# Key sums of a linear-attention block: three column blocks summed with 32-column weights of ones, four token tiles in four partition quarters

## The chip, the core and the metric

The kernel runs on one core of one Trainium2 chip. The metric is the time of one execution in microseconds on the device; the median of three runs is used. A profiled execution has a span (first to last instruction) and a time of its own, which also holds what lies around the span.

## What is computed

A transformer block on 2048 tokens of width 640: layer norm, linear attention with 32 heads of 20, residual, layer norm, a gated MLP of width 1728, residual. The kernel computes the output and the gradients of the input and of five weight matrices. What matters here is one sum in the attention:

```
pq, pk = phi(q), phi(k)               # phi(t) = where(t > 0, t + 1, exp(t)) + 1e-6
kv  = einsum("bhsd,bhse->bhde", pk, v)
z   = einsum("bhsd->bhd", pk)         # key sums: over all 2048 tokens, one number per column
num = einsum("bhqd,bhde->bhqe", pq, kv)
den = einsum("bhqd,bhd->bhq", pq, z)[..., None] + 1e-6
o   = num / den
```

`z` has 640 numbers. The denominators need it beside every token, so it is wanted as a row of 640, the same in all 128 partitions.

## The kernel before

Tokens lie in 16 tiles of 128 (`ST = 16`), the width in 5 column blocks of 128 (`DT = 5`). `pk_all` holds phi of the keys, 128 tokens in the partitions, 16 tiles x 640 columns in each. The order of the work on every engine is written out by hand.

The loop at L521 to L564 goes over the 16 token tiles: it computes the keys on TensorE (`p1_mm`, L267), phi on ScalarE and VectorE, and in between some of the queries and the products `macc` (`m_part`, L422: `pk` transposed times the normalized input). Behind the loop, L579 to L630 finish `macc` block by block, while the queries and the first denominators are computed.

The key sums come in two ways. For blocks 0 and 1, `x_ext` carries a column of ones behind the input (memset at L447), so that the products of L422 give the sums as one more column of the accumulator; `m_end` copies that column to `Z` (L431). For blocks 2, 3 and 4, `z_late` (L330) makes them with matmuls of its own: for each of 16 token tiles and 3 blocks, the 128x128 tile of `pk_all` is loaded as weights and one column of ones moves through (L334). The three sums come out as three columns, one number per partition. ScalarE copies them to `Z` (L336).

`z_diag` (L326) then spreads each column of `Z` on a diagonal: VectorE multiplies the identity by it (L328) into a region of `hx`. `z_rows` (L340) multiplies a 128x128 matrix of ones by each diagonal (L344), which gives the row of sums in all partitions; ScalarE copies the rows to `Zb` (L347). The products `pq * Zb` (`r_prod`, L359, on GpSimd) and the sums over heads (`r_red`, L366, on VectorE) follow.

The order around the change:

```
579  q_tile(4)
...
582  phi_rest()
583  m_part(1, (14, 15))
584  m_end(1)
...
589  z_late((2, 3, 4), big())
590  m_part(2, range(10))
591  z_rows(((0, 1), (2, 3, 4)), ps.tile([P, 2, 512], F32, name="bigx", tag="big", bufs=2))
592  r_prod(0)
593  q_tile(5)
```

The accumulators of `m_part(2)` are the two of block 0 again (L419), so its first matmuls wait until ScalarE has copied these out (L429, L431). Later steps that the prediction speaks of: the weight product `Wp`, made on TensorE (`f2_wT`, L696), copied by ScalarE and VectorE (L699) and transposed by DMA on SyncE's queue (L700); the transposes of the scaled queries (`r_T`, L377); and the last column tile of the MLP gradient (`ghh_chunk`, L401), where 64 weight columns are used at a time and two halves of the tokens go to partitions 0 to 63 and 64 to 127 of one accumulator.

Of the kernel before, what the change touches and what calls it, by code (L numbers as in the profile page):

```python
# [9 lines left out]
P = 128  # L10
BF16 = mybir.dt.bfloat16
# [9 lines left out]
ST, DT = S // P, D // P  # L21
# [34 lines left out]
def kernel(  # L56
# [19 lines left out]
    V, A, T, G, SY = nc.vector, nc.scalar, nc.tensor, nc.gpsimd, nc.sync  # L76
# [27 lines left out]
    def pool(name, side="left", space=None):  # L104
        kw = dict(space=space) if space is not None else dict(side=side)
        return tc.alloc_tile_pool(name=name, bufs=1, reuse_waits="tile", **kw)

    cp = pool("cp")
# [10 lines left out]
    ones = cp.tile([P, P], BF16, name="ones")  # L119
# [115 lines left out]
    pk_all = p1.tile([P, ST, D], BF16, name="pk_all", tag="pk")  # L235
    mT = U1.tile([P, DT, D], BF16, name="mT", tag="MW")
    Z = cp.tile([P, DT], F32, name="Z")
# [14 lines left out]
    def p1_tr(t, parts=((0, DT),)):  # L252
        xn = x_sb[:, t, :]
        for a, b in parts:
            tr = ps.tile([P, DT, P], BF16, name="tr", bufs=2)
            for c in range(a, b):
                T.transpose(tr[:, c, :], xn[:, c * P:(c + 1) * P], ident[:])

            A.copy(out=pqT[:, a:b, t * P:(t + 1) * P], in_=tr[:, a:b, :])  # L259
# [13 lines left out]
    def p1_mm(t, n0, between=None, halves=None):  # L273
        acc = p1_acc() if halves is None else None
        for j in range(2):
            p1_half(acc[:, j, 0:HD] if halves is None else halves[j][:, 0:HD], t, n0 + j * HD)
            if j == 0 and between is not None:
                between()
        return acc
# [27 lines left out]
    hx = ph.tile([P, FT * W], BF16, name="hx", tag="H1")[:, 0:11 * D].rearrange("p (t n) -> p t n", n=D)  # L307
# [14 lines left out]
        phi(p1_mm(t, 0), pqs[t], t)  # L322

    dz = {}

    def z_diag(m):  # L326
        dz[m] = hx[:, 10, m * P:(m + 1) * P]
        V.tensor_scalar(out=dz[m], in0=ident[:], scalar1=Z[:, m:m + 1], scalar2=None, op0=ALU.mult)  # L328

    def z_late(ms, acc):  # L330

        for t in range(ST):
            for i, m in enumerate(ms):
                T.matmul(acc[:, i:i + 1], lhsT=pk_all[:, t, m * P:(m + 1) * P], rhs=ones[:, 0:1],  # L334
                         start=(t == 0 and i == 0), stop=(t == ST - 1), skip_group_check=True)
        A.copy(out=Z[:, ms[0]:ms[-1] + 1], in_=acc[:, 0:len(ms)])  # L336
        for m in ms:
            z_diag(m)

    def z_rows(parts, acc):  # L340

        for k, ms in enumerate(parts):
            for i, m in enumerate(ms):
                T.matmul(acc[:, k, i * P:(i + 1) * P], lhsT=ones[:], rhs=dz[m], start=(i == 0), stop=True,  # L344
                         skip_group_check=True)
        for k, ms in enumerate(parts):
            A.copy(out=Zb[:, ms[0] * P:(ms[-1] + 1) * P], in_=acc[:, k, 0:len(ms) * P])  # L347
# [173 lines left out]
    for t in range(ST):  # L521
        first = None
        if t < RAW:
# [11 lines left out]
            k = p1_mm(t, D, between, kh)  # L535
            act(0, 1)
            act(1, 1)
        else:
            k = p1_mm(t, D, (lambda: p1_tr(t + 1)) if t + 1 < XT_DMA else None)
# [47 lines left out]
    for go in w13[4:]:  # L587
        go()
    z_late((2, 3, 4), big())
    m_part(2, range(10))  # L590
    z_rows(((0, 1), (2, 3, 4)), ps.tile([P, 2, 512], F32, name="bigx", tag="big", bufs=2))
    r_prod(0)
    q_tile(5)
# [384 lines left out]
    for c in range(SC):  # L978
# [9 lines left out]
        for fc in range(FT):  # L988
# [23 lines left out]
            if c == SC - 1 and fc in (1, 2, 5, 6):  # L1012
                i = (1, 2, 5, 6).index(fc)
# [61 lines left out]
    for fc in range(FT - 1):  # L1075
        b, i = divmod(fc, 4)
        if fc == FT - 2:
            gw2_tail()
        acc = ps.tile([P, 2, 512], F32, name="gw", bufs=4)
        for j in range(2):  # L1080
            for t in range(ST):
                T.matmul(acc[:, j, 0:HD], lhsT=hb[b][:, t, i * P:(i + 1) * P], rhs=g2[:, t, j * HD:(j + 1) * HD],  # L1082
                         start=(t == 0), stop=(t == ST - 1))
# [35 lines left out]
    def b_ghn(t):  # L1119

        acc = ps.tile([P, 2, 512], F32, name="ghn", bufs=2)
        n = 0
        lo = (t % 2) * P
        for k in range(NG):
            rhs = wT[0][:, k, :] if k < FT else wT[1][:, k - FT, :]
            for j in range(2):
                T.matmul(acc[:, j, 0:HD], lhsT=ggb[t // 2][:, k, lo:lo + P], rhs=rhs[:, j * HD:(j + 1) * HD],  # L1127
                         start=(k == 0), stop=(k == NG - 1))
                n += 1
                if n % 9 == 0 and n < 54:  # L1130
                    yield
        b_ln(acc, t)
# [109 lines left out]
    for t in range(ST):  # L1242
        g = b_ghn(t)
# [13 lines left out]
        if t >= 1:  # L1257
# [3 lines left out]
            if t <= 2 * DT:  # L1261
                n = (t - 1) % DT
# [95 lines left out]
    def d_acc():  # L1358
        return ps.tile([P, 2, 512], F32, name="dkv", bufs=3)

    def square(lhsT, rhs, i):

        acc = d_acc()
        for c, a, b, bank, off, first in SQ:
            T.matmul(acc[:, bank, off:off + (b - a) * DH], lhsT=lhsT[:, c, i * P:(i + 1) * P],
                     rhs=rhs[:, c, a * DH:b * DH], start=first, stop=True, skip_group_check=True)
        return acc
# [12 lines left out]
    for m, (a, b) in enumerate(M_H):  # L1380
        n = (b - a) * DH
        acc = ps.tile([P, 512], F32, name="gkvT", tag="dkv", bufs=3)
        for c in range(DT):
            T.matmul(acc[:, 0:n], lhsT=woT[:, c, m * P:(m + 1) * P], rhs=QT[:, c, a * DH:b * DH], start=(c == 0),
                     stop=(c == DT - 1))
# [38 lines left out]
    acc = d_acc()  # L1424
    for m in range(DT):
        T.matmul(acc[:, m // 4, m % 4 * P:(m % 4 + 1) * P], lhsT=ones[:], rhs=gzd[:, m, :], start=(m % 4 == 0),
                 stop=True, skip_group_check=True)
# [3 lines left out]
    for t in range(ST):  # L1431
        c, i = divmod(t, TPC)
        u = t // 2
        acc = d_acc()
        for j in range(2):
            for k in range(DT):
                T.matmul(acc[:, j, 0:HD], lhsT=xnT[c][:, k, i * P:(i + 1) * P], rhs=gm[:, k, j * HD:(j + 1) * HD],  # L1437
                         start=(k == 0), stop=(k == DT - 1))
# [7 lines left out]
        if t in (2, 5, 8, 11, 14):  # L1446
            n = t // 3
            acc = square(mN, gkv_b, n)
            k = (4, 0, 1, 2, 3)[n]
# [7 lines left out]
        if t in (6, 8, 10, 12):  # L1457
            n = t // 2 - 3
# [20 lines left out]
    def both_grads(m, f0, f1):  # L1479

        return [(max(f0, lo) - f0, min(f1, lo + F) - f0, out[:, m, max(f0, lo) - lo:min(f1, lo + F) - lo])
                for lo, out in ((0, out4S), (F, out5S)) if max(f0, lo) < min(f1, lo + F)]
# [55 lines left out]
    for i, (f0, f1) in enumerate(blocks):  # L1538
        n = f1 - f0
        for m in range(DT):  # L1540
            last = (i, m) == (len(blocks) - 1, DT - 1)
            for a, b in ((0, n - P), (n - P, n)) if last else ((0, n),):
                c = (a + b) // 2
                halves = ((a, c), (c, b)) if i * DT + m < 6 else ((a, b),)
                out = [(x + y - a, z + y - a, to) for y, w in halves for x, z, to in both_grads(m, f0 + y, f0 + w)]
# [38 lines left out]
```

## Time and profile before

| what | value |
|---|---|
| median of 3 runs | 821.91 us (821.35 to 822.22) |
| profiled execution | 822.18 us, its span 820.4 us |
| TensorE matmuls (PE) | 812.7 us busy, 5437 instructions |
| TensorE weight loads (PEld) | 512.9 us busy, 5464 instructions |
| VectorE (DVE) | 453.0 us busy |
| ScalarE (ACT) | 325.3 us busy |
| GpSimd (POOL) | 131.0 us busy |
| DMA | 157.57 MB, mean 192 GB/s |

PE and PEld overlap: a weight load can run while a matmul streams. Busy time of PE counts overlapping matmuls once. The chain of work that ended last is followed back from the last instruction, at each step to what released it or to the instruction before it on its engine; its pieces are listed with start and length. In groups of instructions "128*128 128x320" is a matmul with weights of 128 rows by 128 columns whose output is 128 partitions by 320 columns. Some matmul records can be missing from a trace.

### The profile page before, as it was taken

What the parts mean: (1) busy time and instruction counts of PE and PEld (TensorE: products, weight loads), DVE (VectorE), ACT (ScalarE), POOL (GpSimd) and SP (SyncE); (2) the same over time, 40 slices, a digit from 0 to 9 for tenths busy, and PEclk for the clock granted to TensorE, in tenths of its full rate; (3) what the DMA queues carried; (4) which work ended last, traced back from release to release, by engine and by line L of the source; (5) the groups of instructions that cost most, each with busy time, mean ns of one, the idle gap of its engine ahead of it and who ended that gap; (6) DMA issues with size and microseconds to landing.
All of it is one profiled execution on the core that took longest, in us unless ns stands there. A gap on an engine that the chain in (4) does not pass through costs nothing.

```text
span 820.4 us, 14028 instructions
## 1 busy us (share of the span) xinstructions
PE 812.7 (99%) x5437; PEld 512.9 (63%) x5464; DVE 453.0 (55%) x976; ACT 325.3 (40%) x605; POOL 131.0 (16%) x193
## 2 busy tenths in 40 slices
PE   8999999999999999999999999999999999999998
PEld 6677544555555545777777777777777777544444
DVE  7859887999898566300057777772781544200000
ACT  7856788655565666011122212222212334211111
POOL 2233333323322212100001111110220000000000
PEclk9999999999999999999999999999999999999999
DMA  9999989696485556999777897359996898978761
GB/s 231 252 271 237 210 233 321 191 240 156 140 218 156 159 188 167 223 263 257 220 173 178 207 204 187 72 113 180 240 210 125 166 197 158 238 166 191 167 138 37
DMA packets 322690, 157.57 MB, mean 192 GB/s; under 512 B 241728, under 2 KB 315872, under 8 KB 322624
## 3 DMA queue, kind: packets, MB, share of 16 engines
q1 hardware_dynamic: 279712, 115.85, 63.5%
q10 hardware_dynamic: 35584, 16.34, 9.3%
q0 software_dynamic: 7328, 24.48, 8.9%
q8 instruction: 43, 0.70, 0.4%
q14 instruction: 23, 0.19, 0.1%
HBM read 47.09 MB, written 51.13 MB: 120 GB/s over the span
## 4 chain that ended last, share of the span: by engine, by line
PE 95%; DMA 3%; DVE 1%; ACT 1%; issue 0%; SPq 0%; DVEq 0%
PE mm L387 20%; PE job L1331 20%; PE ghn L1127 14%; PE gxn L1500 8%; PE gw L1082 7%; PE o L895 4%; PE o L841 3%; PE big L267 3%; PE gwo L1215 3%; PE gr L1184 3%; PE dkv L1437 3%; PE macc L422 2%; PE at L648 2%; PE mm L267 1%; DMA pqT<-pql 1%; DMA wqkv<-in_A_wqkv_dram 1%
## 5 line engine op out<-in xcount | busy, mean ns | idle before, releaser
L1331 PE MATMUL job<-gb,hnN 128*128 128x496 bf16 (+3 forms) x576 | 116.8, 366 | 0.0
L1127 PEld LDWEIGHTS <-ggb 128*128 128x128 bf16 x864 | 84.5, 98 | 32.9
L1331 PEld LDWEIGHTS <-hnN 128*128 128x128 bf16 x576 | 55.7, 98 | 61.1
L387 PE MATMUL mm<-pqT,w 128*128 128x512 bf16 x397 | 93.2, 379 | 0.5
L387 PEld LDWEIGHTS <-w 128*128 128x128 bf16 x540 | 52.5, 98 | 63.1 <-issue 1.1
L1335 ACT CAST obs<-job 128x496 bf16<-128x496 f32 (+4 forms) x56 | 28.5, 509 | 123.7 <-PE job L1331 123.7
L1127 PE MATMUL ghn<-w13a,ggb 128*128 128x320 bf16 x448 | 63.5, 299 | 0.0
L1142 DVE SCALAR_TENSOR_TENSOR wb<-gs,hnb 128x640 f32<-128x640 bf16 x16 | 13.2, 826 | 89.8 <-ACT gs L1139 89.8
L1127 PE MATMUL ghn<-w13b,ggb 128*128 128x320 bf16 x416 | 61.4, 299 | 0.0
L387 PE MATMUL mm<-g2T,w2T 128*128 128x512 bf16 x227 | 58.5, 379 | 0.6
L1082 PE MATMUL gw<-g,hb 128*128 128x320 bf16 x416 | 56.8, 299 | 0.0
L1192 POOL TENSOR_TENSOR sz<-Zb,g_h 128x640 f32<-128x640 bf16 x16 | 20.2, 1260 | 197.7 <-DVE g_h L1193 197.7
L1082 PEld LDWEIGHTS <-hb 128*128 128x128 bf16 x416 | 40.6, 98 | 16.0 <-issue 0.3
L412 ACT CAST ghh<-mm 128x512 bf16<-128x512 f32 x48 | 28.3, 589 | 43.5 <-PE mm L387 36.8
L778 ACT ACTIVATE sig<-mm 128x512 bf16<-128x512 f32 x56 | 33.7, 602 | 25.7 <-PE mm L387 22.0
L1139 ACT ACTIVATE gs<-ghn 128x640 bf16<-128x640 f32 x16 | 11.2, 703 | 78.8 <-PE ghn L1127 58.4
L387 PEld LDWEIGHTS <-w2T 128*128 128x128 bf16 x260 | 25.3, 98 | 23.3
L267 PEld LDWEIGHTS <-pqT 128*128 128x128 bf16 x320 | 30.4, 98 | 14.2 <-ACT pqT L259 0.9
L267 PE MATMUL big<-wqkv,pqT 128*128 128x320 bf16 x250 | 38.4, 299 | 0.5 <-DMA pqT<-x_sb 0.3
L1331 PEld LDWEIGHTS <-g 128*128 128x128 bf16 x320 | 31.0, 98 | 11.6
L814 DVE TENSOR_TENSOR gate<-gate,sig 128x1024 bf16<-128x1024 bf16 x28 | 19.3, 690 | 33.7 <-ACT gate L789 33.6
L789 ACT CAST gate<-mm 128x512 bf16<-128x512 f32 x56 | 33.6, 600 | 4.1 <-DMA gg_d<-gate 4.0
(216 smaller groups left out, 1372.7 us busy)
## 6 DMA issues: line engine op xcount, KB each, us to landing
hh_d<-hhT SPq DMA_DIRECT2D x24, 256.0 KB, 2.8
gg_d<-gate POOLq DMA_DIRECT2D x24, 256.0 KB, 4.6
gg_d<-ghh POOLq DMA_DIRECT2D x24, 256.0 KB, 3.9
ggb<-gg_d SPq DMA_DIRECT2D x6, 896.0 KB, 5.3
ggb<-gg_d ACTq DMA_DIRECT2D x6, 832.0 KB, 5.7
x_sb<-in_A_x_dram SPq DMA_DIRECT2D x6, 640.0 KB, 5.7
ggb<-gg_d SPq DMA_DIRECT2D x2, 1728.0 KB, 12.7
pk_d<-pk_all SPq DMA_DIRECT2D x4, 640.0 KB, 8.0
```

The lines of the kernel that those rows point to most:

```text
L267: T.matmul(acc, lhsT=pqT[:, c, t * P:(t + 1) * P], rhs=wqkv[:, c, n0:n0 + HD], start=(c == 0), stop=(c == DT - 1))
L387: T.matmul(acc[:], lhsT=w[:, c, fc * P:(fc + 1) * P], rhs=rhs[:, c, :], start=(c == 0), stop=(c == DT - 1))
L412: A.copy(out=ghh[n // 2][:, n % 2, :], in_=acc[:])
L778: A.activation(sig[:, i, :], gp[:], AF.Sigmoid)
L789: A.copy(out=gate[:, i, :], in_=gp[:])
L841: T.matmul(accs[i, j][:, 0:HD], lhsT=hhT[c][:, fc, i * P:(i + 1) * P], rhs=w2[:, fc, j * HD:(j + 1) * HD], start=(first and fc == 0), stop ...
L895: T.matmul(o2["ps"][:, 0:HD], lhsT=hhT[c][:, fc, i * P:(i + 1) * P], rhs=w2[:, fc, j * HD:(j + 1) * HD], start=(fc == 0), stop=(fc == FT - 1))
L1082: T.matmul(acc[:, j, 0:HD], lhsT=hb[b][:, t, i * P:(i + 1) * P], rhs=g2[:, t, j * HD:(j + 1) * HD], start=(t == 0), stop=(t == ST - 1))
L1127: T.matmul(acc[:, j, 0:HD], lhsT=ggb[t // 2][:, k, lo:lo + P], rhs=rhs[:, j * HD:(j + 1) * HD], start=(k == 0), stop=(k == NG - 1))
L1331: T.matmul(acc[:, 0:n], lhsT=lhs[:, t, m * P:(m + 1) * P], rhs=rhs(t), start=(t == 0), stop=(t == ST - 1))
L1335: A.copy(out=ob, in_=acc[:, 0:n])
L1500: T.matmul(acc[:, j, 0:HD], lhsT=g, rhs=wqT[:, k, j * HD:(j + 1) * HD], start=(k == 0), stop=(k == 14))
```

## The change

`z_late` no longer loads the keys as weights. It loads 32 columns of ones as weights and moves 384 columns of the keys (the three blocks side by side) through them. The output has 32 partitions, all with the same partial sum. Four token tiles in turn go to the four quarters of 32 partitions of one accumulator, and each quarter sums four token tiles. The accumulator is copied as a whole, 128x384 in bf16, to the region of `hx` where the three diagonals were. `z_rows` then adds the four quarters and spreads the sum over all partitions with one matmul, whose weights are a new 128x128 constant `zone` of 1/32 (each quarter holds its partial sum 32 times). Blocks 0 and 1 stay on diagonals.

```diff
+    NZ = 4
+    ZG = P // NZ
+    zone = cp.tile([P, P], BF16, name="zone")
+    V.memset(zone[:], 1.0 / ZG)
...
     def z_late(ms, acc):
 
-        for t in range(ST):
-            for i, m in enumerate(ms):
-                T.matmul(acc[:, i:i + 1], lhsT=pk_all[:, t, m * P:(m + 1) * P], rhs=ones[:, 0:1],
-                         start=(t == 0 and i == 0), stop=(t == ST - 1), skip_group_check=True)
-        A.copy(out=Z[:, ms[0]:ms[-1] + 1], in_=acc[:, 0:len(ms)])
-        for m in ms:
-            z_diag(m)
+        n = len(ms) * P
+        for t in range(0, ST, NZ):
+            for g in range(NZ):
+                T.matmul(acc[g * ZG:(g + 1) * ZG, 0:n], lhsT=ones[:, 0:ZG], rhs=pk_all[:, t + g, ms[0] * P:ms[0] * P + n],
+                         start=(t == 0), stop=(t == ST - NZ))
+        zs = dz[ms] = hx[:, 10, ms[0] * P:ms[0] * P + n]
+        A.copy(out=zs, in_=acc[:, 0:n])
 
     def z_rows(parts, acc):
 
         for k, ms in enumerate(parts):
+            if ms in dz:
+                T.matmul(acc[:, k, 0:len(ms) * P], lhsT=zone[:], rhs=dz[ms], start=True, stop=True)
+                continue
             for i, m in enumerate(ms):
                 T.matmul(acc[:, k, i * P:(i + 1) * P], lhsT=ones[:], rhs=dz[m], start=(i == 0), stop=True,
                          skip_group_check=True)
```

The lines behind the change move down by 7 in the new kernel. The memset of `zone` stands between the memsets of the small constants (L120 to L124) and the pad memsets (L446, L447) on VectorE.

## The prediction

> **What bounds the kernel now.** I read the page first: busy time, then the slices.
>
> ```profile
> span 820.4 us, 14028 instructions
> PE 812.7 (99%) x5437; PEld 512.9 (63%) x5464; DVE 453.0 (55%) x976; ACT 325.3 (40%) x605; POOL 131.0 (16%) x193
> PE   8999999999999999999999999999999999999998
> PEclk9999999999999999999999999999999999999999
> ```
>
> TensorE's matmul side is busy in every slice, at the full granted clock. A busy PE is not yet a PE at its peak, so the second view is the chain of work that ended last, in order of time, around the changed place (columns: start, length, what).
>
> ```profile
> 50.73 1.36 PE macc L422 x10
> 52.10 1.18 PE bigx L334 x48
> 53.28 2.74 PE macc L422 x20
> 56.02 0.28 PE bigx L344 x5
> 56.29 1.36 PE big L267 x10
> ...
> 97.56 7.87 PE mm L387 x36
> ...
> 132.77 0.67 PE mm L401 x10
> ```
>
> The changed matmuls (L334, the late key sums, and L344, the broadcast of the sums) are pieces of this chain, end to end with their neighbours. So a nanosecond of TensorE saved here is a nanosecond of the chain, as far as 85.8 us, where the chain goes through transfers for the first time after this point. The prices: 10 matmuls of 320 columns in 1.36 us are 136 ns each, 36 of 512 columns in 7.87 us are 219 ns each, 5 of 128 columns in 0.28 us are 56 ns each. All three give 0.43 ns a column, so a matmul of 384 columns, which the profile lacks, is 384 x 0.427 = 164 ns in a stream, and one of 256 columns 109 ns.
>
> The third view is the two source lines themselves: L334, which goes, and L401, the only line of this kernel whose weights are narrower than 128 columns and whose outputs lie in different partitions of one accumulator.
>
> ```profile
> L334 PEld LDWEIGHTS <-pk_all x48: 94/96/98, 51.8 to 53.1; 128*128 128x128 bf16 x48
> L401 PEld LDWEIGHTS <-w2T x40: 106/110/111, 132.7 to 258.7; 128*64 128x64 bf16 x40
> L401 PE MATMUL mm<-g2T,w2T x40: 272/273/298, 132.7 to 258.8; 128*64 128x256 bf16 x40
> ```
>
> L334: 48 pairs of a weight load and a one-column matmul took 1.18 us, 24.6 ns a pair, although one load takes 96 ns by itself. The loads overlap; this part is already cheap, and that is what the change competes with. L401: 10 took 0.67 us in the chain, and the chain's later piece of 20 (at 257.89 us) took 1.21 us. The second ten thus cost 0.54 us, 54 ns each, half of the 109 ns that 256 columns need. Two such matmuls, to partitions 0 to 63 and 64 to 127, run side by side, their 110 ns loads hidden. What is left, 0.67 - 0.54 = 0.13 us, is the price of going into this form and out again.
>
> **The change part by part.**
> *Out:* 48 pairs of L334, 1.18 us of the chain. *In:* 16 pairs, weights of 32 columns of ones, 384 columns moving, 4 adjacent matmuls to 4 partition quarters. Four abreast has no row here, so it is bounded. If all four run together as the two of L401 do: 4 groups x 164 ns = 0.66 us, and 0.13 us for in and out: 0.79 us, which is 0.39 us less. If only two run together: 8 x 164 + 130 = 1.44 us, 0.26 us more. If none do: 16 x 164 + 130 = 2.75 us, 1.57 us more. Without the switching cost the best is 0.66 us, 0.52 us less. I take the four abreast, the full 0.39 us, because the row nearest in kind shows perfect overlap for its width and its loads, at 110 ns, hidden under 109 ns of moving.
>
> Against this the Trainium skill has a sentence: "TensorE: Matmul & The Clock Gate", Part 3, The mechanism, has a load overlap matmuls in flight only when the row group differs, and all four quarters here use the same rows. By that rule no load hides, and the block would be 16 x (110 + 164) ns = 4.4 us with L401's load time. L401 contradicts it: 20 loads of 110 ns are 2.2 us, and the whole piece took 1.21 us. The same page's table of measured packing gives three column tiles a speedup of 2.38; scaled to four (3.2, an estimate from that page) the block would be 2.62 / 3.2 = 0.83 us and 0.13 us for switching, 0.22 us less than before instead of 0.39.
>
> *The next matmuls:* L422 (block 2's first) waits for ScalarE to have emptied the accumulator of block 0. From the timeline:
>
> ```profile
> 51.95 0.76 ACT L429 CAST hx<-macc 128x320 bf16<-128x320 f32 x2
> 52.58 0.21 ACT L431 COPY Z<-macc 128x1 f32<-128x1 f32 x1
> 52.63 0.81 ACT L429 CAST hx<-macc 128x320 bf16<-128x320 f32 x2
> 53.31 0.26 ACT L336 COPY Z<-bigx 128x3 f32<-128x3 f32 x1
> ```
>
> That accumulator is free at 52.58 + 0.21 = 52.79 us. The new block ends at 52.10 + 0.79 = 52.89 us, just behind it, so nothing waits; but the wait stands ready: of a still shorter block only 0.1 us more plus the one matmul ahead of the waiting one (136 ns) could be had.
>
> *ScalarE:* L336 copies 384 columns instead of 3: 485 ns by the row of L347, which has that very shape (128x384), instead of 263 ns, 0.22 us more. It starts when the second L431 is issued, 53.31 us, and ends at 53.8 us; its reader, the third matmul of the broadcast, comes at about 55.7 us. Queued behind it on ScalarE is only L347, which waited 2.75 us for TensorE anyway. Cost 0; without that cover, 0.22 us.
>
> *VectorE:* three of the five diagonals of L328 (about 250 ns each) go; TensorE reached their readers (55.85 us) 1.4 us after the last was done (54.49 us), so 0 gained. The new constant is one 128x128 memset, 165 ns by the row of L120, ahead of the two pad memsets. VectorE then sat 1.82 us for the first rows of x before its first statistics (3.12 us), so 0; without the wait 0.17 us, once. The warm-up matmuls need only the memsets ahead of it.
>
> *Broadcast, L344:* five matmuls of 128 columns (0.28 us) become two of 128 and one of 384: 2 x 56 + 164 = 0.28 us. 0. The order on SyncE and GpSimd, and every transfer, is the same in both programs, so no queue is passed.
>
> *Sum to 85.8 us:* -0.39 us.
>
> *What lies behind.* The first transfer in the chain is the last Wp transpose (4.34 us, to 90.14), then a pqT transpose (5.93 us). Their queue, SyncE, waited 3.2 us at L700 for VectorE's copy of a TensorE result, so it is paced by TensorE and moves with it. But DMA is near full there:
>
> ```profile
> core 0: us, PE busy (x) PEld busy (x) DVE busy (x) ACT busy (x) POOL busy (x), PEclk, DMA share, GB/s
> 74.00:86.00 12.00, 11.95 (x115) 9.13 (x114) 10.31 (x28) 11.12 (x31) 2.43 (x4) 1.00 0.84 173
> 86.00:98.00 12.00, 11.62 (x88) 7.48 (x87) 10.67 (x30) 7.50 (x15) 5.44 (x9) 1.00 1.00 231
> 98.00:140.00 42.00, 41.79 (x211) 20.33 (x214) 35.82 (x69) 34.28 (x68) 14.36 (x20) 1.00 0.98 267
> ```
>
> TensorE's idle time from 86 to 98 us is 0.38 us (12.00 - 11.62). If transfers that do not move end these waits, the idle time grows by what was saved and the saving is 0. Bounds 0 and 0.39; I take 0.39, since the last waits before that stage go back to TensorE's results. Against the profiled execution (822.18 us, span 820.4, 1.8 us around it): span 820.0, time 821.8. The median of the runs is 0.27 us below that execution, so by the median 821.91 - 0.39 = 821.5 us.
>
> **The rivals.** A measurement of this kernel tells 0.2% (1.64 us) from no change: faster is under 820.27 us, slower over 823.55.
> *Swallowed (821.9 us):* the transfers at 90 to 97 us, in a stage with a DMA share of 1.00, arrive when they did. For: TensorE waited 0.47 us there for Wp. Against: the transposes are issued behind TensorE's results.
> *Two abreast (822.2 us) or none (823.5 us):* for it, only a pair is ever shown together, and four abreast read four different sets of columns at once; against it, the pair shows no loss at all.
> *Slower, the loads come out:* with weights changed for every quarter, each 32-column load waits for the matmul ahead. All in line: 16 x 274 + 130 ns = 4.5 us, 3.3 us more, 825.2 us. If only each group's four loads come out, 4 x (4 x 110 + 164) + 130 = 2.5 us, 1.4 us more, 823.3 us. For it: a load of 64 columns takes 110 ns, longer than one of 128 (96 to 98), so narrow loads are not cheap, and four must hide under one 164 ns stream where L401 hides two under 109. It counts as slower from (1.18 + 1.64) / 16 = 176 ns a matmul on. Against: 24.6 ns a pair at L334 shows loads overlapping one another.
> *Faster by more than the block:* both touched pieces are 1.46 us in all, less than 1.64, so this needs later waits to shrink as well. TensorE's idle time behind is 0.38 us at 86 to 98, 0.21 at 98 to 140; saving these too gives 821.91 - 0.39 - 0.59 = 820.9 us, and more only by later transfers falling otherwise, for which nothing in the profile speaks.
>
> **How the numbers follow.** Forecast, four abreast and passed on in the main: 0.55, with its own range 821.2 to 821.9. Swallowed 0.14, two abreast 0.07, none abreast or grouped loads at 823.3 to 823.5 0.04: these four lie within 0.2%, 0.80. Slower by exposed loads, or by later transfers falling worse: 0.13. Faster by over 0.2%: 0.07. The time is that of the forecast, 821.5. The range goes from the best block, 0.52 us less, lowered by the spread of the runs (821.91 - 821.35 = 0.56): 820.8, up to none abreast, 823.5; the two outer cases, 0.20, are left out.
>
> **What would show it.** In the profile after: the 16 matmuls of the key sums as one chain piece of 0.7 to 0.9 us, block 2's first L422 piece beginning near 52.9 us with no idle time ahead of it, the copy at about 485 ns ending before 54 us, the broadcast at 0.28 us, and everything from there to 85 us some 0.4 us earlier. A piece of 1.4 us means two abreast, 2.5 us or more means that nothing overlaps or that loads come out. If the piece is short and the span the same, look at the wait for Wp near 90 us: an idle time grown from 0.47 to about 0.9 us is the swallowed case. The forecast is wrong if the piece is longer than 1.18 us, or if the span moves by more than 1 us while the piece moves by 0.4.

## The result and the profile after

The changed kernel takes 823.90 us (median of 21 runs, 822.67 to 826.83) against 822.15 us before (21 runs in the same sessions, 821.35 to 823.78): a ratio of 1.0022, 95% interval 1.0016 to 1.0028. It is slower by 0.2%, and its runs spread over 4.2 us instead of 2.4. The profiled execution took 823.22 us and has a span of 821.4 us, against 820.4 before.

The key sums did what they should. The two changed lines in the profile after (lines behind the change have numbers 7 higher than before: L429 was L422, L160 stays), and the chain of work that ended last, in order of time ("..." stands for pieces left out):

```profile
L339 PEld LDWEIGHTS <-ones x16: 93/96/97, 51.8 to 52.1; 128*32 128x32 bf16 x16
L339 PE MATMUL bigx<-pk_all,ones x16: 325/326/337, 51.8 to 52.3; 128*32 128x384 bf16 x16
```
```profile
51.82 0.76 PE bigx L339 x16
52.59 2.82 PE macc L429 x20
55.41 0.11 PE bigx L351 x2
55.52 0.16 PE bigx L348
...
88.64 8.55 DMA pqT<-pql
...
97.32 0.46 DVE hn L160
```

The 16 matmuls are one piece of 0.76 us instead of 1.18, and the next piece follows without a gap. But the chain now goes through a transfer of 8.55 us that ends at 97.19 us: the transpose of the scaled queries of token tile 5 (`r_T(5)`). The windows of the two kernels, before and then after, show the stage in which the time went (columns: window, its length, busy time of PE, PEld, DVE, ACT, POOL, granted clock, DMA share, GB/s):

```profile
86.00:98.00 12.00, 11.62 (x88) 7.48 (x87) 10.67 (x30) 7.50 (x15) 5.44 (x9) 1.00 1.00 231
```
```profile
86.00:98.00 12.00, 9.77 (x74) 6.45 (x73) 9.09 (x26) 6.13 (x12) 4.90 (x8) 1.00 1.07 205
```

TensorE's idle time there is 2.23 us instead of 0.38. Who waited for whom in the kernel after, from 80 to 100 us (total, times, longest; `hn` is the output of the second layer norm for a token tile):

```profile
PE trh L757 <- DVE hn L160: 2.2, 1, 2.2
DVE hn L160 <- DMA pqT<-pql: 2.1, 1, 2.1
```

The third `hn` tile (`f2_hn(2)`) takes one of the four `pql` buffers, the one whose scaled queries `r_T(5)` transposes. VectorE can't write it before that transfer has read it, and TensorE waits for VectorE. In the kernel before, the same two waits and the start of `hn` in the chain were:

```profile
PE trh L750 <- DVE hn L160: 0.3, 1, 0.3
DVE hn L160 <- DMA pqT<-pql: 0.2, 1, 0.2
96.25 0.46 DVE hn L160
```

`hn` started at 96.25 us before and at 97.32 us after: 1.07 us later, although the transfer that it waits for was issued earlier. That is the whole of the 1.0 us between the two spans. The rest of the 1.75 us between the medians is not in this trace; the last section comes back to it.

The order on SyncE's queue is unchanged, but not its pace. First before, then after:

```profile
87.05 2.23 SPq L377 DMA_TRANSPOSE pqT<-pql  x1
89.71 0.38 SPq L186 DMA_DIRECT2D x_sb<-in_A_x_dram  x1
90.20 2.22 SPq L377 DMA_TRANSPOSE pqT<-pql  x1
```
```profile
86.43 1.28 SPq L384 DMA_TRANSPOSE pqT<-pql  x1
88.15 0.38 SPq L186 DMA_DIRECT2D x_sb<-in_A_x_dram  x1
88.64 1.36 SPq L384 DMA_TRANSPOSE pqT<-pql  x1
```

After, `r_T(5)` is issued 1.56 us sooner and lands 1.07 us later. The packet records of the trace say why. Counted per half microsecond by their end: packets of 256 B on SyncE's queue (transposes) and packets of the stores on GpSimd's queue (here mostly the 640 KB to `pq_d`).

```
             before                      after
from us   transposes    stores       transposes    stores
 91.0          0          47              1          31
 91.5          0          29             16          40
 92.0          0          41             34          38
 92.5          0          31             29          28
 93.0          0          21            107          13
 93.5          0          17            173           3
 94.0        128           4            190           4
 94.5        291           0             63           1
 95.0        309           0              0           0
 95.5        457           0              8           0
 96.0        565           0             19           0
 96.5        170           0            516           0
one 16 KB fetch at      87.79                     94.79
```

`r_T(5)` has 128 x 640 x 2 / 256 = 640 packets. Before, they run behind the store, undisturbed, from 94 us on. After, they start beside the store and crawl; 613 transpose packets are done when, at 94.79 us, a 16 KB read on queue q8 (the page's kind "instruction") begins. Then hardly a transpose moves for a microsecond and a half: 27 end between 95.5 and 96.5 us, and 24 packets that start between 94.85 and 94.99 us, 11 of them small completion packets of 4 B, end at 96.5. (The records don't name the transfer of a packet; some of the 613 can belong to the next transpose in the queue.)

The rows of that queue on the two pages, before and after (queue, kind: packets, MB, share of 16 engines):

```profile
q8 instruction: 43, 0.70, 0.4%
```
```profile
q8 instruction: 42, 0.69, 0.4%
```

These reads go with TensorE's instructions: there are 43 in each of the five kernels here with 10,928 weight loads and matmuls (5464 of each; some matmul records are missing on the page) and 42 in each of the seven with 10,860 to 10,866. The change has 68 TensorE instructions fewer (32 pairs at L334, two at L344). So all later fetches come at other places of the program: the sixth at 94.79 us instead of 87.79. In the five kernels with the larger number it starts between 87.7 and 89.6 us, in the other seven between 93.3 and 100.4.

SyncE's pace goes with that too. In the five kernels with the early fetch the two transposes took 2.07 to 2.34 us each to issue, in the other seven 1.28 to 1.37. So a moved fetch comes with two differences: the transposes are issued faster and run beside the store instead of behind it, and a fetch falls into them. Why the pace changes was not tried.

### The profile page after: what moved, and what is told of

It reads as the page before. It is cut to its first block, busy times and chain, and to the rows that moved or that the text cites. A ratio compares the mean times of both kernels' runs of the same rounds, so it can differ in the third digit from the quotient of the medians.

```text
span 821.4 us, 13958 instructions
## 1 busy us (share of the span) xinstructions
PE 812.8 (99%) x5403; PEld 512.6 (62%) x5430; DVE 452.4 (55%) x974; ACT 325.2 (40%) x605; POOL 131.1 (16%) x193
## 4 chain that ended last, share of the span: by engine, by line
PE 96%; DMA 1%; DVE 1%; ACT 1%; issue 0%; POOL 0%; DVEq 0%
PE mm L394 20%; PE job L1338 19%; PE ghn L1134 14%; PE gxn L1507 8%; PE gw L1089 7%; PE big L267 4%; PE o L902 4%; PE o L848 3%; PE gwo L1222 3%; PE macc L429 3%; PE dkv L1444 3%; PE gr L1191 3%; PE at L655 2%; DMA pqT<-pql 1%; PE dkv L1372 1%; PE gp L394 1%
```

## The experiments

The first theory, F: the moved instruction fetch makes the loss. The rival, P: being 0.4 us earlier makes it, whatever the fetch does. Each kernel ran in five rounds beside the kernel before.

**Give back the 68 instructions in the warm-up, at the same work.**
```diff
-            T.matmul(warm[:, 0:P], lhsT=ones[:], rhs=ones[:], ...)
+            T.matmul(warm[:, 0:wide], lhsT=ones[:], rhs=ones[:, 0:wide], ...)
-    warm_up(WARM, ps.tile(...))
+    warm_up(2 * WARM, ps.tile(...), P // 2)
```


> The changed kernel with its opening warm-up cut finer: 68 matmuls of 64 columns instead of 34 of 128, so 68 more TensorE instructions (as many as the kernel before has) at the same warm-up work; nothing else. Theory F (the 68 instructions that the change saves move the points at which TensorE's next 16 KB of instructions are fetched; one fetch, at 94.8 us in the changed kernel's trace against 87.8 before, now falls into the pqT transpose that the third hn waits for, all transposes in flight stand still for 1.6 us, and TensorE waits 2.2 us): the fetch is back near 87 us, the wait for hn is 0.2 to 0.5 us, time 821.5 to 822.0, below before by about 0.4. Theory P (being 0.4 us earlier by itself makes the transfers at 88 to 97 us fall badly): as the changed kernel, 823.4 to 824.5, wait near 2.2 us.

Measured 823.15 us (before 821.97; ratio 1.0010, 1.0002 to 1.0019). The fetch was back at 88.60 us, SyncE's two transposes took 2.14 and 2.12 us to issue as in the kernel before, and `hn` waited 0.2 us. But the time was not 821.5 to 822.0. The delay lay ahead of the key sums, which began at 53.26 us (52.10 in the kernel before): a transpose of `x_sb` took 6.66 us from 25.72 us on (5.32 from 25.80 on before), and TensorE idled 0.96 us between 31 and 51 us (0.17 before, 0.01 in the changed kernel). The early fetches had moved too (10.7 and 24.9 us instead of 16.4 and 32.1); that they made this delay is likely, not shown. F's wait was met, its time missed.

**Make it as late as before, with two wide matmuls behind the key sums.**
```diff
-    z_late((2, 3, 4), big())
+    zb = ps.tile([P, 2, 512], F32, name="bigx", tag="big", bufs=2)
+    z_late((2, 3, 4), zb[:, 0])
+    for _ in range(2):
+        T.matmul(zb[:, 1], lhsT=ones[:], rhs=pk_all[:, 0, 0:512], start=True, stop=True)
```


> The changed kernel with two matmuls of 512 columns into an unused bank behind the key sums, about 0.44 us of TensorE: everything behind runs as late as in the kernel before, with 4 more instructions only. Theory P (phase): the transfers fall as before, time 821.9 to 822.4. Theory F (instruction fetch): the fetch stays near 95 us, the hn wait stays near 2 us or moves little, time 823.8 to 824.9.

Measured 826.62 us (6 runs, 824.74 to 827.86; ratio 1.0049, 1.0036 to 1.0061), more than either theory gave. `hn` waited 2.9 us. It speaks against P, but not cleanly: the added matmuls waited for ScalarE's copy of the key sums, which lie in the same tile, so TensorE idled 1.19 us between 51 and 86 us and ran later than before, not as late.

**Take 62 instructions out of the kernel before, at the same work.**
```diff
-    warm_up(WARM, ps.tile(...))
+    warm_up(8, warm, 4 * P)
+    warm_up(1, warm, 2 * P)
-    warm_up(8, p1_acc()[:, 0])
+    warm_up(2, p1_acc()[:, 0], 4 * P)
```
(`warm_up` moves `wide` columns of ones, read with stride 0.)

> The kernel before, its key sums untouched, with the warm-up cut coarser: 8 matmuls of 512 columns and one of 256 for 34 of 128, and 2 of 512 for 8 of 128, the same columns in 62 TensorE instructions fewer. Theory F: the fetch moves from 87.8 to about 94 us and the slowdown appears without the change: wait for the third hn 1.5 to 2.5 us, time 823.5 to 825. Theory P: no change, 821.9 to 822.4. If the transposes stand still a little earlier or later than in the changed kernel, the loss can be smaller, 822.5 to 823.5.

Measured 825.00 us (7 runs, 823.53 to 827.36; ratio 1.0034, 1.0019 to 1.0049). The key sums are the old ones. The fetch came at 95.12 us and the wait appeared; what VectorE's `hn` waited for (us, times), and the stage's window:

```profile
  DMA pqT<-pql: 2.1, 1
```
```profile
86.00:99.00 13.00, 10.77 (x82) 7.39 (x81) 10.07 (x28) 6.57 (x13) 5.13 (x9) 0.96 0.99 211
```

The loss needs nothing of the change but its missing instructions. This speaks against P: TensorE was as busy from 51 to 86 us as in the kernel before (34.95 of 35 us in both). It doesn't end it, because SyncE issued the first of the two transposes 0.3 us earlier (86.75 us against 87.05; 86.43 in the changed kernel).

**Give the third hn a buffer of its own.**
```diff
-        hn[t] = (pf.tile([P, D], BF16, name="hn", tag="pql", bufs=4) if t == 2 else
+        hn[t] = (hx[:, 10, :] if t == 2 else
```


> The changed kernel with the third hn tile in the region of hx that held the key sums (free since 56 us) instead of the buffer of the scaled queries of tile 5, so that it no longer waits for their transpose. Both theories: the wait at 95 to 97 us goes, time 821.3 to 821.9, below before by 0.3 to 0.8. If it stays near 823.9, the loss does not go through this wait.

Measured 821.41 us (11 runs, 820.97 to 821.98) against 821.97: ratio 0.9989, 0.9980 to 0.9998. The transfers still collide (a fetch at 96.88 us), but nobody waits. It is a little faster than the kernel before and 2.5 us faster than the changed kernel was in its own session. The same edit on the kernel before:

> The kernel before with the third hn tile in the free region of hx, the edit of a_ownbuf alone. F: there is only a wait of 0.2 to 0.5 us to take away here, so 821.5 to 821.9, and a_ownbuf (821.41, against a before of 821.97) stays below it by the 0.4 us of the key sums. If this edit is worth 0.5 us or more by itself (821.4 or less), the key sums' own gain does not reach the end.

Measured 822.31 us against 822.36 (ratio 1.0005, 0.9995 to 1.0015): no gain that can be told, and above the 821.5 to 821.9 expected; the kernel before was slower in that session too (822.36 against 821.97). In the kernel before this wait cost next to nothing. Against the kernel before of its own session, the changed kernel with this edit gains 0.56 us and the kernel before with it 0.05. The difference of 0.51 us fits the 0.42 us of the key sums, so they seem to arrive; a run of the two side by side, which would show it, was not made.

**The instructions given back behind the early fetches, with work added.** 34 pairs of a load and a one-column matmul, first behind the key sums:
```diff
+    for _ in range(34):
+        T.matmul(zb[:, 1, 0:1], lhsT=pk_all[:, 0, 0:P], rhs=ones[:, 0:1], start=True, stop=True)
```


> The changed kernel with 34 pairs of a weight load and a one-column matmul into an unused bank right behind the key sums: work added, nothing else. They give back the 68 TensorE instructions there, so that all instruction fetches before 51 us stay where they were (unlike a_more68, which moved the early ones too), and cost 34 x 24.6 ns = 0.84 us, so TensorE is 0.42 us later than in the kernel before. Theory F (fetch): the fetch comes near 88 us, the wait for the third hn is 0.2 to 0.5 us, time 822.2 to 822.9, a microsecond or more BELOW the changed kernel (823.9) in spite of the added work. Theory P (phase) or any theory without the fetch: 823.9 plus 0.8, about 824.7, or near a_late's 826.

Measured 823.96 us (ratio 1.0023, 1.0014 to 1.0032), a miss in time for the reason of the second experiment: the pairs waited 1.1 us for ScalarE. The `hn` wait was gone, the fetch at 89.61 us. Both were run again with the added matmuls ahead of the key sums, where nothing holds them.

> a_pairs34 with its 34 added pairs ahead of the key sums instead of behind them: in a_pairs34 they stood behind ScalarE's copy of the key sums (same tile), and TensorE waited 1 us for it. Now no wait; TensorE should be 0.42 us later than in the kernel before (0.84 added, 0.42 saved), with the kernel before's number of instructions. F: fetch near 88 us, hn wait 0 to 0.5 us, 822.3 to 823.0. P or any theory without the fetch: 824.0 to 824.9.

> a_late with its two matmuls of 512 columns ahead of the key sums, for the same reason: TensorE is then as late as in the kernel before at 55 us (within 0.1 us), with 64 instructions fewer than it. F: fetch near 95 us, hn wait 1.5 to 3 us, 823.7 to 825. P: as the kernel before, 821.9 to 822.5. It should come out ABOVE a_pairs34b, which does 0.4 us more work.

Measured 823.29 us with the 34 pairs (822.27 to 829.02, ratio 1.0010, 0.9995 to 1.0024) and 825.75 us with the two wide matmuls (822.96 to 828.72, ratio 1.0037, 1.0024 to 1.0051). Both medians lie above what was expected (822.3 to 823.0 and 823.7 to 825); five of the 11 runs with the pairs are within 822.27 to 822.64. The kernel with more added work, 0.83 us of it against 0.43, is the faster one by 2.5 us in the median. The chain's pieces, with the pairs and then with the wide matmuls:

```profile
51.85 0.83 PE bigx L598 x34
52.68 0.76 PE bigx L339 x16
```
```profile
52.40 0.43 PE bigx L598 x2
52.83 0.76 PE bigx L339 x16
```

SyncE's queue in the two, in the same order:

```profile
87.29 2.12 SPq L384 DMA_TRANSPOSE pqT<-pql  x1
...
90.33 2.12 SPq L384 DMA_TRANSPOSE pqT<-pql  x1
```
```profile
87.44 1.28 SPq L384 DMA_TRANSPOSE pqT<-pql  x1
...
89.63 1.34 SPq L384 DMA_TRANSPOSE pqT<-pql  x1
```

TensorE's wait in the two, and for the second the window behind it:

```profile
PE trh L760 <- DVE hn L160: 0.4, 1, 0.4
```
```profile
PE trh L760 <- DVE hn L160: 4.5, 1, 4.5
```
```profile
99.00:140.00 41.00, 38.84 (x197) 19.18 (x198) 32.65 (x66) 29.79 (x58) 11.71 (x16) 0.92 0.86 230
```

The key sums start 0.15 us apart and the first transpose is issued 0.15 us apart. The two programs differ only in the added matmuls, 34 pairs or 2, with the fetches at 88.04 and 98.44 us, and the wait is 0.4 or 4.5 us. P falls here: with the two wide matmuls nothing is earlier than in the kernel before (key sums from 52.83 us on against 52.10, first transpose at 87.44 against 87.05), and the loss is there. The profiled execution with the wide matmuls is the slowest of its 12 (828.72 us), so its usual wait may well be shorter than 4.5 us. The long wait also costs clock: the mean granted clock is 0.92 in the 41 us behind it, 3.3 us of full clock.

**Move the store that the transpose crawls beside.**
```diff
-        ... (f2_m_out,), (q_out, 10, 14), (load_w2T, 8 * P, 10 * P), ...
+        ... (f2_m_out,), (load_w2T, 8 * P, 10 * P), ...
-        ... (f2_hn, 1), (f2_half, 3, 1),
+        ... (f2_hn, 1), (q_out, 10, 14), (f2_half, 3, 1),
```


> The changed kernel, buffers and instruction counts untouched, with one store moved: the 640 KB of queries to pq_d (GpSimd's queue, issued at 88.6 us, just ahead of the pqT transpose that the third hn waits for) goes out behind the second hn instead, near 94 us. The packet records of the changed kernel show the transpose's packets crawling beside this store from 91.5 to 94.5 us and then standing still at the fetch. If the loss needs both (F, refined: the store slows the transpose so that it is still in flight when the fetch at 94.8 us comes), the transpose lands before 93 us, the hn wait is 0 to 0.3 us and the time 821.3 to 822.0, the fetch being where it was. If the fetch or the missing instructions cost 2 us in some other way, the time stays near 823.9. Risk: the store now ends near 100 us and can hold the buffers that follow it, up to 1 us.

Measured 821.68 us (821.20 to 822.26; ratio 0.9992, 0.9983 to 1.0001).

```profile
PE trh L757 <- DVE hn L160: 0.2, 1, 0.2
```

VectorE no longer waits for the transpose, though the fetch (93.3 us) still falls into it and it lands at 95.3 us, not before 93. So the fetch alone does not make the loss: the store must slow the transpose as well. In the changed kernel the fetch then makes most of the wait: 613 packets are done when it begins at 94.79 us, and VectorE begins to wait at 95.2. But the crawl can make a wait by itself. In the profiled execution with the two wide matmuls ahead, VectorE waited from 96.2 us on (4.4 us), 2.2 us of it before that kernel's fetch began at 98.44 us. How much of the loss each of the two makes in other executions is open.

**All 16 matmuls in one quarter** (on the kernel with the own buffer).
```diff
-                T.matmul(acc[g * ZG:(g + 1) * ZG, 0:n], ...
+                T.matmul(acc[0:ZG, 0:n], ...
```
The copy takes 32 partitions and the broadcast sums over 32 rows.

> a_ownbuf with all 16 matmuls of 32 weight columns in one quarter (partitions 0 to 31) instead of four, and the broadcast over 32 rows: the same instructions, none side by side. The prediction's terms: 16 x 164 + 130 ns = 2.75 us for the piece instead of 0.76, so time 823.4, some 2.0 us above a_ownbuf. If the quarters do not matter, the piece stays near 0.8 us and the time near 821.4. If narrow loads come out between the matmuls, the piece is 3 to 4.5 us.

```profile
52.96 2.70 PE bigx L339 x16
55.66 2.82 PE macc L429 x20
```

The piece is 2.70 us and the time 823.34 us, 1.93 us above the four quarters (821.41, in another session), for 1.94 us more in the piece. Four abreast is a speedup of 2.70 / 0.76 = 3.6. The Trainium skill's table ("TensorE: Matmul & The Clock Gate", Part 3, Measured speedup vs the span model) has 2.38 for three column tiles; no run here used three.

## Why the prediction was wrong

- *The block.* 0.79 us foretold from L401's pairs, 0.76 measured; without overlap 2.75 foretold, 2.70 measured. Four abreast, loads hidden: right, and the rule that a load overlaps only across row groups, weighed there, did not hold: the 16 loads of 96 ns alone are 1.5 us, twice the piece of 0.76 us.
- *The next matmuls, the memset, the broadcast.* L429 follows at 52.59 us without a gap; the memset of `zone` lies at 1.06 us, and VectorE still waits 1.71 us for x behind it; the broadcast is 0.11 + 0.16 = 0.27 us against 0.28. Right.
- *The copy.* 485 ns foretold, 580 measured (53.04 to 53.62 us); hidden as said, so mis-sized without effect.
- *Up to 85 us.* Some 0.4 us earlier was foretold; the issue of the Wp transposes began at 79.90 us instead of 80.51, of which 0.27 us stood already ahead of the key sums (their neighbour began at 50.46 instead of 50.73). Right.
- *What lies behind: the step that failed.* It gave the stage at 86 to 98 us the bounds "0 and 0.39", as though transfers could only swallow the saving. TensorE's idle time there grew by 1.85 us. Under it lies the sentence that "The order on SyncE and GpSimd, and every transfer, is the same in both programs, so no queue is passed". The instruction fetches are transfers too: the page's row of q8 counts 43 of them. Taking out 68 instructions of TensorE moved those behind. The step counted instructions only by their time, and took a change at a place with a DMA share of 1.00 as unable to hurt.
- *The rivals.* The one that happened, later transfers falling worse, stood only as half a clause among the slower cases, without place or price. The place was named for another case (the wait at 90 us for Wp); the wait that decided was that of `hn` for `pqT`, 0.2 us in the profile before, in a chain piece of 5.93 us which the prediction itself quoted. Here the profile before gave no upper bound for a transfer that lies in the chain of a busy stage: 5.93 us there, 8.55 after.

## What to carry to other kernels

Count the instructions that a change takes away or adds on TensorE, not only their time: they moved the later instruction fetches here, and a fetch that met DMA transposes in flight often went with a standstill of a microsecond and more. Where a saving runs into a wait for a transfer in a busy stage, bound it on the loss side too, and look at which buffer makes the consumer wait: here one tile in a free region took the wait away and let the saving through, to 821.41 us. To test a suspicion of this kind, keep the work and change only the number of instructions, at a place behind those fetches that are to stay where they are, and where nothing waits.

## What the runs showed of the hardware that I had not expected

Transposes in flight often stand still at an instruction fetch. In the packet records of the 12 kernels here, 188 fetches found transposes at work (at least 40 of their packets on SyncE's queue started in the half microsecond ahead). The longest transpose packet from there until 1.2 us after the fetch took over 0.9 us in 111 of these, 1.11 us in the median. At 1032 other times with as many transposes (one looked at every 2 us, 3 us and more from any instruction read), it was over 0.9 us at 20, and 0.068 us in the median. Why it is so was not tried.

Beside a store on GpSimd's queue, the transposes of the changed kernel advanced about packet for packet: 16, 34 and 29 against the store's 40, 38 and 28 in the three half microseconds from 91.5 us on, where alone they do some 300 to 570. That agrees with the Trainium skill ("DMA: Bandwidth & Descriptors", Queues, rings and completion order): each engine goes round its queues packet by packet. By that a small packet gets no more turns than a large one. The mix is not always so even: with the own buffer it was 147 and 208 against 23 and 12 in the two half microseconds from 91.5 us on.

A wait of TensorE also has a step in its price. Six of the 21 runs of the changed kernel have a mean granted clock of 0.998 instead of 1.000, and these six are its slowest (824.66 us and up, median 825.1; the other 15 have 823.29, 1.14 us above the kernel before). The skill ("TensorE: Matmul & The Clock Gate", Part 1) has the clock halved after an idle window of about 3.4 us. The traces show the halving after shorter waits than that. The profiled changed kernel waited 2.2 us and kept its clock at 1.00. The kernel with 62 instructions fewer waited 2.2 us as well, and its clock was 0.50 for the 3.4 us behind; this is the 0.96 in its window above. After the 3.0 us that TensorE waited in the second experiment it was 0.50 for 3.4 us, after the 4.5 us for 6.8. So here a wait of 2.2 us can cost the clock or not, and half of 3.4 us, 1.7 us, is about what separates the six runs from the others.
